# Converting the first weights 1024 wide without GpSimd, and squaring on ScalarE alone

## The chip, the core and the metric

One core of a Trainium2 chip. The metric is the time of one execution on the device in microseconds. An engine's queue runs in order; the program gives each engine its own order, and semaphores hold an instruction until its inputs are written and its output buffer is free.

## The reference

Three layers in a row on 3072 tokens of 512 features:

```python
# retention: per token t and head, decay gamma_h = 1 - 2^(-5-h)
state = gamma * state + outer(k[t], v[t]);  y[t] = scale * q[t] @ state
# first MLP, d_ff = 2048
r = maximum(x @ w_in, 0);  x2 = (s * r * r + b) @ w_out
# second MLP: 8 experts, each takes exactly 384 tokens by sorted gate logits
out[mask] = maximum(x2[mask] @ w1[e], 0) @ w2[e]
```

The outputs are compared as float32. The weights `w_in` and `w_out` of the first MLP are drawn as float64 and not cast, so they come to the chip as 64-bit words (`w64`, seen as int64), and the kernel has to make 32-bit numbers of them.

## The kernel before

Float32 products are made from two rounded parts: each operand is split into a high part (`fp32r`) and the remainder, and three matmuls (high x high, high x low, low x high) stand for one.

**Weights of the first MLP.** `w64` holds 16 features (slices of 128 of `d_ff`), each with two pieces of 128 x 512 words (`w_in`, `w_out`): 32 pieces `n`, feature `f = n // 2`. `conv_load` (line 228) fetches a piece of 512 KB into one of six buffers, on SP's queue. `conv_gen` (line 233) converts one piece at a time: from the upper word `hi32` VectorE takes the exponent shifted by three bits (line 262), joins the sign (266), sets very small numbers to zero with the help of a square made by ScalarE (239, 269), takes the bare power of two (275) and multiplies it by the lower word (279). For the piece before, ScalarE rounds the number to the high part `h` (249), GpSimd subtracts (251) and adds the lower word's share to give the low part `l` (253). Each `yield` tells a planner (`Weave`, `Side`) how much time the step is charged (`CY`); the planner issues a step when its due time has come, between the units of TensorE's work. `conv_until` forces conversion forward when a unit needs weights that are not yet issued.

**Order.** At first three blocks of 256 tokens go through the retention (`attn`, six chunks of 128 tokens), with a few pieces of conversion in between (`PRO`, `PN`). The chunks' loads and the first raw pieces stand on SP's queue in the order written near line 571. VectorE masks (344) and makes remainders (377), GpSimd scales each chunk by decays (201, 204). Then the *wide* stage: `moe1((0, 1, 2), ...)` takes feature by feature, and for each the three blocks. A *unit* is `h_unit` (12 matmuls, line 425, 256 wide, then `relu` on ScalarE into `r`, line 428) and, two units later, `x_unit` (six matmuls, line 458, 512 wide). Conversion runs beside it. Then comes the *narrow* stage: blocks 3 to 9 one after the other with the next block's retention and the gate logits (line 481) beside them; then the last two blocks as a pair (`h_pair`), and after that the expert stage.

**Squares.** `r_split` makes the two parts of `r * r`. In the wide stage ScalarE squares and rounds in one instruction (436), VectorE makes the unrounded square from `r` and the accumulator bank `ph` (440), GpSimd subtracts (441). In the later stages `low_parts` issues VectorE's square (447) and its subtraction (448) at the start of the next unit.

Buffers: `tmp` has six, used by conversion and by the logits; `loads` holds the later chunks of q, k and v in `q0` and `q2`, two of each, where the raw pieces lie as well; `stage` has two `sa` and two `sb`.

Of the kernel before, what the change touches and what calls it, by code (L numbers as in the profile page):

```python
# [35 lines left out]
TINY_WORD = 1.125 * 2.0 ** -15  # L36
# [45 lines left out]
def kernel(  # L82
# [19 lines left out]
    CY=(560, 890),  # L102
# [72 lines left out]
    def load_chunk(j):  # L175
        if j < CPB:

            ts = []
            for i in range(4):
                n = 2 * NF - 1 - 2 * j - i // 2  # L180
                tag = ("h", "l")[i % 2] + str(n)
                ts.append(wpool.tile([128, 512], F32, name=f"first{j}_{i}", tag=tag))
            for i in (0, 1, 3, 2):
                SP.dma_start(ts[i], qkv[j, :, i])
                if j == 0 and i in first:
                    first[i]()
            if j:
                load_dec(j)
        else:
            ts = []  # L190
            load_dec(j)
            for i in (0, 2):
                t = loads.tile([128, 2, 512], F32, name=f"q{i}", tag=f"q{i}")
                SP.dma_start(t, qkv[j, :, i:i + 2])
                ts += [t[:, 0, :], t[:, 1, :]]
        QKV[j] = ts
# [28 lines left out]
    NRAW = 6  # L225
    READY = set()

    def conv_load(n):
        pool, tag = ((stage, "sa"), (loads, "q0"), (loads, "q2"))[n // 2 % 3]
        RAW[n] = pool.tile([128, 512], I64, name="raw", tag=tag)  # L230
        SP.dma_start(RAW[n], w64[n // 2, n % 2])

    def conv_gen():
        sq = {}

        def square(n):
            hf = RAW[n].bitcast(F32).rearrange("p (n t) -> p t n", t=2)[:, 1, :]
            sq[n] = tmp.tile([128, 512], F32, name="tmp")
            ACT.activation(sq[n], hf, AF.Square)

        square(0)
        last = None

        def parts(step):
            n, a, p = last
            if step == 0:
                W[n] = (wpool.tile([128, 512], F32R, name=f"h{n}", tag=f"h{n}"),
                        wpool.tile([128, 512], F32R, name=f"l{n}", tag=f"l{n}"))
                ACT.activation(W[n][0], a, AF.Copy)
            elif step == 1:  # L250
                POOL.tensor_tensor(a, a, W[n][0].bitcast(F32), op=OP.subtract)
            else:
                POOL.tensor_tensor(W[n][1], a, p, op=OP.add)  # L253
                READY.add(n)

        for n in range(2 * NF):
            raw = RAW.pop(n)
            hi32 = raw.bitcast(I32).rearrange("p (n t) -> p t n", t=2)[:, 1, :]
            lo32 = raw.bitcast(U32).rearrange("p (n t) -> p t n", t=2)[:, 0, :]
            a = tmp.tile([128, 512], F32, name="tmp")  # L260
            ai = a.bitcast(I32)
            DVE.tensor_scalar(ai, hi32, 3, 0x3FFFFFFF, op0=OP.logical_shift_left, op1=OP.bitwise_and)  # L262
            if last:
                parts(0)
            yield CY[0]
            DVE.scalar_tensor_tensor(ai, hi32, -0x40000000, ai, op0=OP.bitwise_and, op1=OP.bitwise_or)  # L266
            yield CY[1]
            p = sq.pop(n)
            DVE.scalar_tensor_tensor(a, p, TINY_WORD * TINY_WORD, a, op0=OP.is_ge, op1=OP.mult)  # L269
            if last:  # L270
                parts(1)
            if n + 1 < 2 * NF:
                square(n + 1)
            yield CY[1]
            DVE.tensor_scalar(p.bitcast(I32), ai, -0x800000, None, op0=OP.bitwise_and)
            yield CY[0]
            if last:
                parts(2)
            DVE.scalar_tensor_tensor(p, lo32, 2.0 ** -52, p, op0=OP.mult, op1=OP.mult)
            if n + NRAW < 2 * NF:  # L280
                conv_load(n + NRAW)
            last = (n, a, p)
            yield CY[1]
        for step in range(3):
            parts(step)
            yield 600
# [129 lines left out]
    def h_unit(blk, f, hb):  # L416
# [12 lines left out]
        return r, ph  # L429
# [3 lines left out]
    def r_split(r, rh, rl, ph=None):  # L433


        ACT.activation(rh, r, AF.Square)  # L436
        if ph is None:
            LOW.append((r, rh, rl))
        else:
            DVE.scalar_tensor_tensor(r, ph, 0.0, r, op0=OP.max, op1=OP.mult)  # L440
            POOL.tensor_tensor(rl, r, rh.bitcast(F32), op=OP.subtract)
        return rh, rl

    def low_parts():
        while LOW:
            r, rh, rl = LOW.pop(0)
            DVE.tensor_tensor(r, r, r, op=OP.mult)  # L447
# [96 lines left out]
    def moe1(blks, xbs, lag, apart=0):  # L544
# [5 lines left out]
        for n in range(len(seq) + lag):  # L550
            if n < len(seq):
                def hu(n=n):
                    f, i = seq[n]
                    conv_until(2 * f + 1)
                    low_parts()
                    r, ph = h_unit(blks[i], f, 2 + n % 2)
                    R2[blks[i], f] = r_split(r, work.tile([128, TB], F32R, name="rh", bufs=3),
                                             work.tile([128, TB], F32R, name="rl", bufs=3),
                                             ph if len(blks) > 1 else None)
# [14 lines left out]
    conv_load(1)  # L574
    SP.dma_start(sb[:, 0:1], bass.AP(tensor=moe_s.tensor, offset=moe_s.offset, ap=[[0, 128], [1, 1]]))
    SP.dma_start(sb[:, 1:2], bass.AP(tensor=moe_b.tensor, offset=moe_b.offset, ap=[[0, 128], [1, 1]]))
    for j in range(2, CPB):
        load_chunk(j)
        conv_load(j)
# [19 lines left out]
    conv_until(2 * NF - 1)  # L599
# [62 lines left out]
    def h_pair(f):  # L662
        rs = []
        for i, blk in enumerate(pair):
            wv.unit(1320, lambda: rs.append(h_unit(blk, f, 2 + i)[0]))
# [512 lines left out]
```

## Time and profile before

| | us |
|---|---|
| median of three runs | 1146.67 (1144.25 to 1148.87) |
| the profiled execution | 1142.75 |
| its span, first to last instruction | 1141.0 |
| TensorE busy in the span | 1016.3 |
| VectorE busy | 875.2 |
| ScalarE busy | 385.1 |
| GpSimd busy | 221.7 |

Busy time is a mean over stages with different limits; what an edit is worth is read in its own stage. Waiting for a semaphore is shown as idle time ahead of an instruction; anything that holds an instruction after its start is inside its duration, so the shortest and the mean duration of one line are read together.

### The profile page before, as it was taken

The numbers are of one execution on the slowest core, as the hardware profiler recorded it, in microseconds if no ns is written. First come the engines' busy times: TensorE is split into PE (matmuls) and PEld (weight loads), VectorE is DVE, ScalarE is ACT, GpSimd is POOL, SyncE is SP. The second block draws the span as 40 slices with busy tenths as digits, with TensorE's granted clock in tenths as the row PEclk, the third lists the DMA queues.
The fourth block names the chain that finished last, engine by engine and source line by source line (L and its number), as shares of the span: only waits on it lengthen the run. The fifth ranks groups of instructions, "written<-read, shape, count | busy, mean of one in ns | idle before, by whom it ended". The sixth has DMA issues, their size and how long they took to land.

```text
span 1141.0 us, 19761 instructions
## 1 busy us (share of the span) xinstructions
PE 1016.3 (89%) x7636; PEld 875.8 (77%) x7636; DVE 875.2 (77%) x2114; ACT 385.1 (34%) x802; POOL 221.7 (19%) x211
## 2 busy tenths in 40 slices
PE   5887877899999999999998999578789888888997
PEld 4766666788889898989897888467677677776786
DVE  3899999669999999999964744667787787867642
ACT  2433333332323323223333331223333443333442
POOL 3777777620000000000000000010111102011211
PEclk8999999999999999999999999869799999999999
DMA  9422222262212121221121000322333333343540
GB/s 323 144 90 92 93 93 82 96 193 75 66 47 75 56 57 56 57 74 58 35 95 32 2 1 11 138 66 85 120 102 121 111 108 134 95 133 116 166 139 28
DMA packets 35040, 104.51 MB, mean 92 GB/s; under 512 B 4737, under 2 KB 5249, under 8 KB 34945
## 3 DMA queue, kind: packets, MB, share of 16 engines
q1 hardware_dynamic: 30528, 89.60, 24.2%
q0 software_dynamic: 3840, 12.59, 3.3%
q8 instruction: 60, 0.98, 0.3%
q10 hardware_dynamic: 576, 1.05, 0.3%
q14 instruction: 36, 0.29, 0.1%
HBM read 90.64 MB, written 12.58 MB: 90 GB/s over the span
## 4 chain that ended last, share of the span: by engine, by line
PE 55%; DVE 23%; issue 11%; DMA 5%; ACT 2%; POOL 2%; SPq 0%; POOLq 0%; DVEq 0%; ACTq 0%
PE b L425 17%; PE b L458 13%; PE b L1012 6%; PE b L1033 5%; PE b L687 3%; DVE tmp L262 3%; DMA big<-x2d,idx 3%; DVE l L990 2%; PE b L794 2%; PE b L358 2%; PE b L368 2%; DVE tmp L266 2%; PE b L338 2%; DVE tmp L269 2%; DVE cmp L787 2%
## 5 line engine op out<-in xcount | busy, mean ns | idle before, releaser
L425 PE MATMUL b<-xh,h 128*128 128x256 f32 x704 | 201.7, 287 | 22.6 <-DVE r L440 20.9
L481 DVE SCALAR_TENSOR_TENSOR scr<-tmp,wg 128x512 bf16<-128x512 f32 x288 | 198.3, 689 | 6.8 <-ACT tmp L468 1.8
L425 PE MATMUL b<-xh,l 128*128 128x256 f32 x704 | 199.5, 283 | 0.9 <-POOL l L253 0.9
L425 PE MATMUL b<-xl,h 128*128 128x256 f32 x704 | 199.3, 283 | 0.0
L425 PEld LDWEIGHTS b<-xh,h 128*128 128x128 f32 x704 | 134.4, 191 | 39.2 <-DVE r L440 31.1
L428 ACT ACTIVATE r<-b 128x256 f32<-128x256 f32 x192 | 73.2, 382 | 253.3 <-PE b L425 225.5
L425 PEld LDWEIGHTS b<-xl,h 128*128 128x128 f32 x704 | 134.4, 191 | 4.8
L425 PEld LDWEIGHTS b<-xh,l 128*128 128x128 f32 x704 | 134.6, 191 | 1.5 <-POOL l L253 1.5
L458 PE MATMUL b<-h,rh 128*128 128x512 f32 x320 | 130.3, 407 | 0.0
L458 PE MATMUL b<-h,rl 128*128 128x512 f32 x320 | 127.1, 397 | 2.7 <-DVE rl L448 2.7
L458 PE MATMUL b<-l,rh 128*128 128x512 f32 x320 | 127.4, 398 | 0.0
L950 POOL DMA_INDIRECT big<-x2d,idx x24 | 26.1, 1088 | 355.1 <-issue 152.6
L1012 PE MATMUL b<-gh,h 128*128 128x384 f32 x256 | 93.1, 364 | 0.0
L1033 PE MATMUL b<-h,hh 128*128 128x512 f32 x192 | 81.0, 422 | 13.3 <-ACT hh L1015 13.3
L1012 PE MATMUL b<-gl,h 128*128 128x384 f32 x256 | 88.2, 344 | 1.7 <-DVE gl L962 1.7
L1012 PE MATMUL b<-gh,l 128*128 128x384 f32 x256 | 87.8, 343 | 0.0
L990 DVE TENSOR_TENSOR l<-eraw,h 128x512 fp32r<-128x512 f32 x128 | 82.3, 684 | 6.6 <-ACT h L989 6.6
L1033 PE MATMUL b<-h,hl 128*128 128x512 f32 x192 | 78.9, 411 | 8.0 <-DVE hl L1021 7.8
L447 DVE TENSOR_TENSOR r<-r 128x256 f32<-128x256 f32 x144 | 60.7, 421 | 25.6 <-ACT h L436 17.9
L1015 ACT ACTIVATE hh<-b 128x384 fp32r<-128x384 f32 x64 | 31.3, 489 | 138.3 <-PE b L1012 138.3
L1033 PE MATMUL b<-l,hh 128*128 128x512 f32 x192 | 76.9, 401 | 0.0
L458 PEld LDWEIGHTS b<-h,rl 128*128 128x128 f32 x320 | 61.0, 191 | 19.3 <-DVE rl L448 5.5
(193 smaller groups left out, 2054.2 us busy)
## 6 DMA issues: line engine op xcount, KB each, us to landing
eraw<-in_w_dram SPq DMA_DIRECT2D x64, 512.0 KB, 3.6
q<-in_qkv_dram SPq DMA_DIRECT2D x36, 512.0 KB, 4.7
raw<-in_w_dram SPq DMA_DIRECT2D x32, 512.0 KB, 3.5
first<-in_qkv_dram SPq DMA_DIRECT2D x24, 256.0 KB, 6.0
qdec<-in_dec_dram SPq DMA_DIRECT2D x24, 256.0 KB, 2.7
x2d<-tmp SPq DMA_DIRECT2D x20, 256.0 KB, 3.8
wg<-in_wgT_dram SPq DMA_DIRECT2D x4, 512.0 KB, 3.6
x2d<-tmp ACTq DMA_DIRECT2D x4, 256.0 KB, 2.0
```

Of the source, the lines that this page charges most:

```text
L262: DVE.tensor_scalar(ai, hi32, 3, 0x3FFFFFFF, op0=OP.logical_shift_left, op1=OP.bitwise_and)
L425: PE.matmul(ph, a[:, ks], b[:, kc, :], start=(n == 0), stop=(n == 3 * KC - 1))
L428: ACT.activation(r, ph, AF.Relu)
L447: DVE.tensor_tensor(r, r, r, op=OP.mult)
L458: PE.matmul(X2[blk][t], a[:, ts], b, start=(f == 0 and i == 0), stop=(f == NF - 1 and i == 2))
L481: DVE.scalar_tensor_tensor(scr, x, 1.0, WG[e], op0=OP.mult, op1=OP.mult, accum_out=of[:, e:e + 1])
L687: PE.matmul(XB[c], a[:, cs], b, start=(f == 0 and i == 0), stop=(f == NF - 1 and i == 2))
L950: POOL.indirect_dma_start(out=xg[:, t, :], out_offset=None, in_=x2d[:, :], in_offset=bass.IndirectOffsetOnAxis(ap=IDX[i][:, t:t + 1], axis=0))
L990: DVE.tensor_tensor(lo, raw[:, a, :], hi.bitcast(F32), op=OP.subtract)
L1012: PE.matmul(PH[0], a[:, ks], b[:, kc, :], start=(kc == 0 and n == 0), stop=(kc == KC - 1 and n == 2))
L1015: ACT.activation(hh, PH[0], AF.Relu)
L1033: PE.matmul(Y[i, t], a[:, ts], b, start=(f == 0 and j == 0), stop=(f == NF2 - 1 and j == 2))
```

## The change

The conversion handles a whole feature (both pieces, 1024 wide) at a time. ScalarE gives the magnitude (`Abs`), VectorE clamps, shifts, joins and makes the lower word's share in place in the raw tile, ScalarE rounds two halves, and VectorE does the subtractions and additions that GpSimd did. Raw features lie in the two buffers of `q`, now one tile of 8 KB for each partition; the first loads and the planner's charges change with it. ScalarE squares `r` in place and rounds it in a second instruction, in all stages; VectorE only subtracts.

```diff
-TINY_WORD = 1.125 * 2.0 ** -15
+ZERO_WORD = 2.0 ** -15
-    CY=(560, 890),
+    CY=(700, 1200, 650),
# load_chunk, chunks from 6 on
+            t = loads.tile([128, 4, 512], F32, name="q")
             for i in (0, 2):
-                t = loads.tile([128, 2, 512], F32, name=f"q{i}", tag=f"q{i}")
-                SP.dma_start(t, qkv[j, :, i:i + 2])
-                ts += [t[:, 0, :], t[:, 1, :]]
+                SP.dma_start(t[:, i:i + 2], qkv[j, :, i:i + 2])
+                ts += [t[:, i, :], t[:, i + 1, :]]
-    def conv_load(n):
...
+    def conv_load(f):
+        RAW[f] = loads.tile([128, 1024], I64, name="raw", tag="q")
+        for i in range(2):
+            SP.dma_start(RAW[f][:, i * 512:(i + 1) * 512], w64[f, i])
     def conv_gen():
...
+        def magnitude(f):
+            mag[f] = stage.tile([128, 1024], F32, name="c", tag="sa")
+            ACT.activation(mag[f], RAW[f].bitcast(F32).rearrange("p (n t) -> p t n", t=2)[:, 1, :], AF.Abs)
+        magnitude(0)
+        for f in range(NF):
+            raw = RAW.pop(f)
+            (_, hi), (_, hf), (lo, _), (lf, _) = (
+                [v[:, t, :] for t in range(2)] for v in
+                (raw.bitcast(d).rearrange("p (n t) -> p t n", t=2) for d in (I32, F32, U32, F32)))
+            c = mag.pop(f)
+            ci = c.bitcast(I32)
+            DVE.tensor_scalar(c, c, ZERO_WORD, None, op0=OP.max)
+            yield CY[0]
+            DVE.tensor_scalar(ci, ci, 3, 0x3FFFFFFF, op0=OP.logical_shift_left, op1=OP.bitwise_and)
+            yield CY[0]
+            DVE.scalar_tensor_tensor(hi, hi, -0x40000000, ci, op0=OP.bitwise_and, op1=OP.bitwise_or)
+            for i in range(2):
...
+                ACT.activation(W[n][0], hf[:, i * 512:(i + 1) * 512], AF.Copy)
+            yield CY[1]
+            DVE.tensor_scalar(ci, hi, -0x800000, None, op0=OP.bitwise_and)
             yield CY[0]
+            DVE.scalar_tensor_tensor(lf, lo, 2.0 ** -52, c, op0=OP.mult, op1=OP.mult)
             yield CY[1]
+            for i in range(2):
+                h, l = W[2 * f + i]
+                part = slice(i * 512, (i + 1) * 512)
+                DVE.tensor_tensor(hf[:, part], hf[:, part], h.bitcast(F32), op=OP.subtract)
+                yield CY[2]
+                DVE.tensor_tensor(l, hf[:, part], lf[:, part], op=OP.add)
+                if f + 1 < NF and not i:
+                    magnitude(f + 1)
+                yield CY[2]
+            if f + 2 < NF:
+                conv_load(f + 2)
+            READY.add(f)
# squares
-    def r_split(r, rh, rl, ph=None):
-        ACT.activation(rh, r, AF.Square)
-        if ph is None:
-            LOW.append((r, rh, rl))
-        else:
-            DVE.scalar_tensor_tensor(r, ph, 0.0, r, op0=OP.max, op1=OP.mult)
-            POOL.tensor_tensor(rl, r, rh.bitcast(F32), op=OP.subtract)
+    def r_split(r, rh, rl):
+        ACT.activation(r, r, AF.Square)
+        ACT.activation(rh, r, AF.Copy)
+        LOW.append((r, rh, rl))
     def low_parts():
         while LOW:
             r, rh, rl = LOW.pop(0)
-            DVE.tensor_tensor(r, r, r, op=OP.mult)
             DVE.tensor_tensor(rl, r, rh.bitcast(F32), op=OP.subtract)
# first loads
     conv_load(0)
     load_chunk(1)
-    conv_load(1)
...
     for j in range(2, CPB):
         load_chunk(j)
-        conv_load(j)
+        if j == 3:
+            conv_load(1)
```

`conv_until(2 * f + 1)` becomes `conv_until(f)`, and `PN = 2` now means feature 2 and no longer piece 2.

## Rows read from the trace of the kernel before

**Rows 1.** The page, busy tenths in 40 slices of 28.5 us, by engine

```profile
PE   5887877899999999999998999578789888888997
DVE  3899999669999999999964744667787787867642
POOL 3777777620000000000000000010111102011211
```

**Rows 2.** Stretches: us, busy PE, PEld, DVE, ACT, POOL (instructions), clock, DMA, GB/s

```profile
47.00:212.00 165.00, 133.23 (x762) 108.92 (x762) 161.55 (x182) 65.22 (x139) 127.03 (x97) 0.97 0.29 93
239.00:600.00 361.00, 360.05 (x2702) 324.05 (x2703) 324.36 (x866) 113.22 (x273) 1.49 (x2) 1.00 0.22 68
600.00:645.00 45.00, 39.85 (x325) 35.05 (x324) 28.71 (x76) 14.64 (x39) 1.22 (x4) 1.00 0.06 20
```

**Rows 3.** Waits from 47 to 215 us: waiter, cause: total us, times, longest

```profile
ACT tmp L239 <- POOL l L253: 60.6, 26, 3.8
PEld b L425 <- DVE r L440: 47.2, 36, 2.5
```

**Rows 4.** Groups from 47 to 215 us: busy us, mean ns, idle before, releasers

```profile
L253 POOL TENSOR_TENSOR l<-tmp 128x512 fp32r<-128x512 f32 x29 | 46.1, 1591 | 1.0
...
L279 DVE SCALAR_TENSOR_TENSOR tmp<-raw,tmp 128x512 f32<-128x512 uint32 x29 | 35.8, 1234 | 0.8
L269 DVE SCALAR_TENSOR_TENSOR tmp<-tmp 128x512 f32<-128x512 f32 x29 | 35.0, 1208 | 0.6
...
L262 DVE TENSOR_SCALAR tmp<-raw 128x512 int32<-128x512 int32 x28 | 33.2, 1184 | 0.0
L266 DVE SCALAR_TENSOR_TENSOR tmp<-raw,tmp 128x512 int32<-128x512 int32 x28 | 28.9, 1034 | 0.8
...
L275 DVE TENSOR_SCALAR tmp<-tmp 128x512 int32<-128x512 int32 x29 | 22.1, 762 | 0.7
L249 ACT ACTIVATE h<-tmp 128x512 fp32r<-128x512 f32 x29 | 18.3, 632 | 35.9 <-DVE tmp L269 35.9
L239 ACT ACTIVATE tmp<-raw 128x512 f32<-128x512 f32 x27 | 18.3, 678 | 60.6 <-POOL l L253 60.6
L436 ACT ACTIVATE rh<-r 128x256 fp32r<-128x256 f32 x43 | 18.0, 418 | 1.4
...
L428 ACT ACTIVATE r<-b 128x256 f32<-128x256 f32 x43 | 15.9, 371 | 3.2 <-PE b L425 3.1
```

**Rows 5.** Single lines, whole span: duration min/median/max; page's group of line 990

```profile
L262 DVE TENSOR_SCALAR tmp<-raw x32: 410/1162/1517, 20.0 to 208.5; 128x512 int32<-128x512 int32 x32
L266 DVE SCALAR_TENSOR_TENSOR tmp<-raw,tmp x32: 674/902/1672, 21.1 to 209.5; 128x512 int32<-128x512 int32 x32
L448 DVE TENSOR_TENSOR rl<-r,rh x112: 424/425/428, 242.0 to 619.2; 128x256 fp32r<-128x256 f32 x112
L990 DVE TENSOR_TENSOR l<-eraw,h 128x512 fp32r<-128x512 f32 x128 | 82.3, 684 | 6.6 <-ACT h L989 6.6
```

**Rows 6.** Timeline, TensorE, the wide stage's first matmul: start, duration

```profile
46.88 0.39 PE L425 MATMUL b<-xh,h 128*128 128x256 f32 x1 [1.41 <-DVE xls L377]
```

**Rows 7.** Chain and timeline at the end of the wide stage, TensorE

```profile
219.16 1.43 PE b L425 x12
...
224.81 1.45 PE b L425 x12
...
230.28 1.16 PE L338 MATMUL b<-q 64*128 64x128 f32 x16
232.11 1.16 PE L338 MATMUL b<-q 64*128 64x128 f32 x16 [0.67 <-POOL q L201]
```

**Rows 8.** Timeline, ScalarE, the only load of function tables

```profile
0.75 1.28 ACT L376 ACT_TABLE_LOAD   x1 [0.75 <-PEq L1165]
```

**Rows 9.** The raw tile, whole span: from issue to landing

```profile
DMA to landing us min/median/max: 3.3/3.5/8.4
```

**Rows 10.** Waits from 583 to 650 us

```profile
PEld b L674 <- DVE l L448: 2.9, 4, 1.4
```

## Blind prediction

> **What bounds the kernel now.** I read the slices of the page first, then a table by stage, then, for the one stage that stands out, the groups by line and the waits. The slices show TensorE at seven or eight tenths until about 228 us, with VectorE at nine from 57 to 200 us and GpSimd at seven; from 240 to 600 us TensorE is at nine [rows 1]. [...] So two stages have two limits. From 47 us on the "wide" stage runs (three token blocks against each feature's weights, while VectorE still converts the weights) and there VectorE is the bound: TensorE's largest wait is on VectorE's `r` of line 440, 47 us in total, and ScalarE sits 61 us behind GpSimd's sums of line 253 [rows 3]. In the later, narrow stage TensorE is the bound.
>
> Why VectorE is full is seen in the groups and in the spread of single lines. Line 262 takes 0.41 us at best and 1.18 us on average in this stage, line 266 0.67 at best, 1.67 at worst and 1.03 on average [rows 4, 5]. The same instruction on the same shape is thus two to three times as long at times, and the time it gains is about that of a GpSimd instruction (1.59 us, line 253) [rows 4]. I read it so: an instruction of VectorE that meets a GpSimd one waits for it inside its own duration.
>
> The wide stage on TensorE starts at 46.88 us [rows 6] and ends where the next stage's line 338 starts, 230.28 us [rows 7]: 183.4 us. When conversion is over, one unit (12 matmuls of line 425 and six of line 458) takes (224.81 - 219.16) / 2 = 2.82 us [rows 7], so 48 units are 135.4 us of TensorE. The most that can be won here is 48 us.
>
> **The change part by part.** *Conversion on VectorE.* Per feature it now issues three one-source instructions, two two-source ones, all 1024 wide, and four subtractions or additions 512 wide. A two-source instruction takes 0.425 us at 256 wide and 0.684 at 512 [rows 5], so 0.26 us for 256 more. The one-source line 262 does 512 in 0.41, that is 512 elements in the time of 256; 1024 wide it is 0.41 + 0.26 = 0.67 us. Two-source at 1024: 0.674 + 0.52 = 1.19 us. Sum: 3 x 0.67 + 2 x 1.19 + 4 x 0.684 = 7.13 us. Before, a feature was ten instructions 512 wide, with GpSimd beside them 2 x (1.18 + 1.03 + 1.21 + 0.76 + 1.23) = 10.8 us [rows 4]. In the wide stage GpSimd now has nothing to do (lines 251, 253 and 441 are gone), so I take the shortest durations, not the means.
>
> *Squares.* Line 440 and GpSimd's line 441 go; ScalarE squares in place and then rounds; VectorE keeps one subtraction of 0.425 us for each unit, issued at the start of the next unit, where its inputs are long ready. TensorE's bank is now released by ScalarE's `relu` alone, which removes the 47 us wait as such; what comes late next is the subtraction, which the second product needs two units later.
>
> *The sum of the wide stage.* The planner charges 7100 for a feature's conversion and 7860 for its three units, so the conversion runs ahead: when the remaining 14 features are through, 14 x 7100 / 2620 = 38 of the 48 units have been issued. VectorE until then: 1.4 us (the last subtractions of feature 1) + 14 x 7.13 + 38 x 0.425 = 117.4 us. Neighbours that don't depend on each other overlap by some 0.07 us; I take 3.5 us off for that and put 2.1% idle on, as in [rows 2] (161.55 of 165): 116.3 us. Ten units are left, 28.2 us, of which TensorE, waiting for the subtraction of two units earlier, can already be ahead by up to 4; I take 2. Together 116.3 + 26.2 = 142.5 us instead of 183.4: 40.9 us less.
>
> *ScalarE.* Per feature: magnitude 1024 wide, about 2 x 0.68 less one start, 1.1 to 1.35 us; two rounded parts, 1.26; three units at 0.37 + 0.42 + 0.42, 3.6 [rows 4]. About 6.1 us in a feature of 8.3: not a bound. A load of function tables is seen once, 1.28 us [rows 8]; I count none for the new function; if it needed its own, 2 x 1.28 us a feature would put ScalarE at 8.7 and cost 14 x 0.4 = 6 us.
>
> *Loads.* Only two raw features are held instead of three, and the load of feature f+2 waits on SP for the last addition of feature f. Behind it on SP stand the next raw loads, and at the end chunks 6 and 7, which take the buffers of features 14 and 15: free near 163 us, wanted near 190. That a later chunk is one tile with two loads costs nothing: both halves were freed and loaded together before. The magnitude on ScalarE, and with it `relu` behind it, waits for the landing. A raw half lands 3.5 us after issue at the median and 8.4 at worst [rows 9]; two issued 0.4 us apart, at about 4 to 5.5, then 1.1 to 1.35 us of magnitude: 6.9 at most, against 8.3 us for a feature. Hidden, at nothing; the rival below prices the worst.
>
> *Start.* The conversion's wider instructions stand between the masks of the attention on VectorE. In program order a 1024-wide pair (0.67 + 1.19) comes ahead of the masks of chunks 2 and 4 and the evictions after them, where half as much came before; the rounded parts stand ahead of an eviction on ScalarE. GpSimd's conversion work leaves its queue, so the last chunk's scaling comes earlier, and chunks 3 and 5 are loaded 512 KB sooner, chunk 1 later; feature 2's load now waits for feature 0, after all the chunks. Between -2 and +3 us; I take +1.5, nearer to the instructions that are certain.
>
> *Later stages.* In the narrow stage 112 multiplications of VectorE (line 447) go, each about as long as line 448's 0.425 us [rows 5], 48 us in all, and 112 roundings of ScalarE come. TensorE is at 360 of 361 us there [rows 2], so this brings nothing; without that cover it would be up to 48 us. Where the last pair of blocks begins TensorE idles 5.15 of 45 us [rows 2], in part behind VectorE's subtraction [rows 10]; with 0.84 us less on VectorE per feature I take 1.8 us. GpSimd's scaling of chunks 6 and 7 no longer queues behind line 441: the 0.67 us wait [rows 7] goes.
>
> Sum: -40.9 + 1.5 - 0.7 - 1.8 = -41.9 us. From the profiled execution, 1142.75 us (span 1141.0), that gives 1100.9. It lies 3.9 us under the median of the runs, so against the median 1146.67 the forecast is 1104.8: 1105 us.
>
> **The rivals.** *TensorE takes over.* If the overlap is larger than I take and no idle comes, VectorE needs no more than TensorE; then the stage is 135.4 us plus the first unit's start, about 1, and the time is 1146.67 - 47 + 1.5 - 2.5 = 1099. For it: 7.13 + 1.28 = 8.41 us against 8.46 a feature. Against: the planner sets conversion ahead, 8.3 us in 7100 of its units.
>
> *The raw load shows.* With landings at the 8.4 us that a row shows, a feature takes 8.4 + 0.4 + 1.1 = 9.9 us instead of 8.3: 14 x 1.6 = 22 us, and the time is 1127. For it: no third buffer. Against: the median 3.5.
>
> *Writes at every second word are slow.* Four instructions of a feature (the join, the lower word's share, two subtractions) now write into the raw tile in place, at every second word, 3072 elements together. No row shows such a write. Reads of this kind cost nothing: line 266 reads at every second word in 0.674 us. Bounds for 512 such elements: nothing more (that row), or 1.00 us more (the same line at its worst, 1.67). I take nothing, since reading and writing walk the same words. At 0.50 us more for each 512 (six a feature, 14 features, 42 us) the gain is used up: at 0.52, each step doubled, 1149, no change; at 1.00, 84 us longer, 1189, slower.
>
> [...]
>
> **How the numbers follow.** Forecast 0.62 (1096 to 1113), TensorE's rival 0.13, the load's 0.14, slow writes 0.11 (of which 0.04 lands within 0.5%). The range from 1093 to 1127 takes in the first three and leaves out slow writes. Half a percent, 5.7 us, is about what a measurement of this kernel can tell from no change. Faster 0.89, same 0.04, slower 0.07.
>
> **What the profile of after would show.** Line by line in the wide stage: one-source conversion at 0.67, two-source at 1.19, subtractions at 0.68 us, minimum and median alike; longer ones at the raw tile's writes alone mean slow writes. GpSimd idle from 50 us to the end of the wide stage. VectorE over 95% busy until about 163 us; if it idles on ScalarE's magnitude, the load shows. The first matmul of line 338 in the next stage near 191 us. From there on the same distances as before. The forecast is wrong if that start comes after 205 us, or if the narrow stage, which now has ScalarE's extra rounding, no longer holds TensorE at full.

## The result and the profile after

| | before | after |
|---|---|---|
| median, us | 1145.46 (1141.52 to 1148.87, four runs) | 1106.49 (1105.77 to 1107.8, four runs) |
| ratio | 1 | 0.9662, 95% interval 0.9628 to 0.9696 |
| span of the profiled execution | 1141.0 | 1104.3 |
| wide stage, start to end | 46.88 to 230.28: 183.4 | 51.83 to 191.96: 140.1 |

The change makes the kernel 3.4% faster; the forecast was 1105 us. Lines of after: 237 is the magnitude, 248, 250, 253, 261 and 263 are VectorE's conversion in the order of the diff, 258 the rounding, 268 and 270 the subtraction and addition; 415, 418, 426, 427, 434 and 444 are `h_unit`'s matmul, `relu`, the square, its rounding, VectorE's subtraction and `x_unit`'s matmul. The attention's matmuls are at 328 and 348, its masks at 334, the eviction at 366 and 367.

The page's slices of after, busy tenths in 40 slices of 27.6 us, answer [rows 1]:

```profile
PE   5699999899999999999999998596888898888997
...
DVE  2899992587887878787726243777868787876642
...
POOL 3200010000000000000000000102020201111211
```

TensorE reaches nine tenths from the third slice on, where before it stood at seven and eight until 228 us; from 36.5 us on GpSimd stands still until it scales chunks 6 and 7, from 161.7 us on. The table of stretches, with busy time of TensorE, weight loads, VectorE, ScalarE and GpSimd (instructions in brackets), granted clock, DMA share and GB/s, answers [rows 2]:

```profile
52.00:98.00 46.00, 46.00 (x302) 42.14 (x303) 44.40 (x67) 30.93 (x66) 0.00 (x0) 1.00 0.40 138
98.00:166.00 68.00, 65.84 (x406) 56.41 (x406) 66.42 (x98) 44.23 (x94) 3.52 (x2) 1.00 0.38 132
166.00:192.00 26.00, 26.00 (x162) 23.07 (x160) 5.94 (x13) 13.34 (x31) 2.47 (x2) 1.00 0.35 118
192.00:204.00 12.00, 8.74 (x122) 7.66 (x121) 4.52 (x9) 3.23 (x8) 2.45 (x2) 0.86 0.65 202
204.00:565.00 361.00, 361.00 (x2708) 326.92 (x2709) 281.24 (x755) 158.76 (x383) 0.21 (x1) 1.00 0.21 66
565.00:610.00 45.00, 41.74 (x346) 37.70 (x346) 23.34 (x62) 22.59 (x59) 1.24 (x4) 1.00 0.07 21
```

The wide stage has three parts now. To 98 us TensorE never idles. To 166 us VectorE is full (66.4 of 68) and TensorE loses 2.2 us to it. From 166 us on conversion is over, VectorE rests, and TensorE alone sets the pace. The stage of 140.1 us thus stands 4.7 us above the 135.4 us that TensorE needs. From 204 to 565 us TensorE is full as it was before. From 192 to 204 us it works only 8.7 of 12.

The conversion's own lines, shortest, median and longest duration in ns, answer [rows 5]; a reader compares the three figures of a line with each other:

```profile
L258 ACT ACTIVATE h<-raw x32: 652/674/707, 26.5 to 161.0; 128x512 fp32r<-128x512 f32 x32
L268 DVE TENSOR_TENSOR raw<-raw,h x32: 680/686/1787, 33.2 to 166.0; 128x512 f32<-128x512 f32 x32
...
L237 ACT ACTIVATE c<-raw x16: 1122/1147/1173, 21.6 to 154.9; 128x1024 f32<-128x1024 f32 x16
L253 DVE SCALAR_TENSOR_TENSOR raw<-raw,c x16: 1217/1226/2168, 24.3 to 159.2; 128x1024 int32<-128x1024 int32 x16
L261 DVE TENSOR_SCALAR c<-raw x16: 683/692/695, 29.0 to 160.7; 128x1024 int32<-128x1024 int32 x16
...
DMA to landing us min/median/max: 3.4/4.3/7.9
```

Shortest and median lie within 4% of each other: what was stretched in [rows 4, 5] is stretched no more. The longest ones lie where GpSimd still scales a chunk: line 253 took 2.17 us at 24.29 us, and line 268 took 1.79 us at 162.55 us, beside the scaling of chunk 6.

Where the 36.7 us between the two spans lie, stretch by stretch, from the first matmul of each stage:

| stretch | before | after | difference |
|---|---|---|---|
| to the start of the wide stage | 46.88 | 51.83 | +4.95 |
| wide stage | 183.4 | 140.1 | -43.3 |
| from its end to the narrow stage | 8.56 | 11.89 | +3.3 |
| the rest | 902.2 | 900.5 | -1.7 |

### The profile page after: what moved, and what is told of

The parts are those of the page before. It is cut to its first block, busy times and chain, and to the rows that moved or that the text cites. A ratio compares the mean times of both kernels' runs of the same rounds, so it can differ in the third digit from the quotient of the medians.

```text
span 1104.3 us, 19566 instructions
## 1 busy us (share of the span) xinstructions
PE 1006.6 (91%) x7636; PEld 877.4 (79%) x7636; DVE 769.6 (70%) x1954; ACT 460.6 (42%) x978; POOL 78.0 (7%) x99
## 4 chain that ended last, share of the span: by engine, by line
PE 66%; DVE 15%; issue 8%; DMA 6%; ACT 3%; POOL 2%; SPq 0%; POOLq 0%; DVEq 0%; ACTq 0%
PE b L415 22%; PE b L444 18%; PE b L997 6%; PE b L1018 5%; PE b L672 3%; DMA big<-x2d,idx 3%; PE b L779 2%; DVE l L975 2%; PE b L348 2%; PE b L358 2%; PE b L328 2%; DVE cmp L772 2%; POOL big L935 2%; DVE raw L268 1%; DVE raw L253 1%
## 5 line engine op out<-in xcount | busy, mean ns | idle before, releaser
L434 DVE TENSOR_TENSOR rl<-r,rh 128x256 fp32r<-128x256 f32 x160 | 68.7, 430 | 46.7 <-ACT rh L427 46.2
L426 ACT ACTIVATE r<-r 128x256 f32<-128x256 f32 x192 | 79.9, 416 | 5.1
```

The costliest lines, as they stand in the source:

```text
L426: ACT.activation(r, r, AF.Square)
L434: DVE.tensor_tensor(rl, r, rh.bitcast(F32), op=OP.subtract)
```

## The experiments

The theory was the prediction's: GpSimd beside VectorE stretches VectorE's instructions, the squares take 0.42 us of VectorE in each unit, and both together bound the wide stage. Rivals were that one part carries all, and that GpSimd's time is no loss but help. Medians are set against runs of before on the same chip, by ratio; where two kernels ran on different chips, their ratios compare better than their medians (that of before was 1142.7 to 1144.9 us on the four chips).

| label | edit, in short | us | ratio (95%) | wide stage, us |
|---|---|---|---|---|
| x1_squares | before, new squares alone | 1127.7 | 0.9858 (0.9835 to 0.988) | 173.0 |
| x12_nopool | before, GpSimd out of the conversion | 1121.7 | 0.9809 (0.9768 to 0.9851) | 160.9 |
| x4_pieces | both of these, still 512 wide | 1100.8 | 0.963 (0.9608 to 0.9652) | 146.1 |
| x11_pieces_new | x4 with the change's arithmetic | 1090.2 | 0.9537 (0.9511 to 0.9563) | 137.4 |
| x2_conversion | after, old squares | 1145.4 | 1.001 (0.9996 to 1.0024) | 173.5 |
| x8_coupled | x2, VectorE subtracts instead of GpSimd | 1148.8 | 1.0044 (1.0015 to 1.0072) | 175.9 |
| x9_vsquare | after, VectorE squares in `low_parts` | 1130.8 | 0.9884 (0.986 to 0.9909) | 160.3 |
| x3_pool | after, 268 and 270 on GpSimd | 1122.1 | 0.9798 (0.9782 to 0.9815) | 155.4 |
| x5_halves | after, chunk 8's halves freed apart | 1103.0 | 0.9642 (0.9615 to 0.9669) | 140.1 |
| x6_start | after, conversion later in the start | 1105.9 | 0.9681 (0.9665 to 0.9697) | 142.5 |
| x13_order | after, chunk 1 loaded ahead of feature 0 | 1103.2 | 0.9656 (0.9619 to 0.9693) | 140.2 |

### The squares alone

```diff
# on before, r_split and low_parts
-        ACT.activation(rh, r, AF.Square)
-        if ph is None:
-            LOW.append((r, rh, rl))
-        else:
-            DVE.scalar_tensor_tensor(r, ph, 0.0, r, op0=OP.max, op1=OP.mult)
-            POOL.tensor_tensor(rl, r, rh.bitcast(F32), op=OP.subtract)
+        ACT.activation(r, r, AF.Square)
+        ACT.activation(rh, r, AF.Copy)
+        LOW.append((r, rh, rl))
...
-            DVE.tensor_tensor(r, r, r, op=OP.mult)
```

> The kernel before with the squares of the change alone (ScalarE squares and rounds, VectorE only subtracts); the conversion stays 512 wide with GpSimd. Theory (VectorE's time in the wide stage sets it, and GpSimd stretches VectorE): a feature cost VectorE 10.8 us where its shortest durations sum to 5.7, a stretch of 5.1 us beside 9.3 us of GpSimd; now GpSimd has 6.4 us a feature, so the stretch is about 3.5, VectorE 5.7 + 3.5 + 1.3 = 10.5 us against 11.6 to 12; the wide stage shrinks by 14 x 1.1 to 1.5 = 15 to 21 us, later stages by 2: about 1126, ratio 0.983. Rival (TensorE's bank, held by VectorE's line 440, is what cost the 47 us wait, and the squares free it): 35 to 40 us, about 1108, ratio 0.967, and nothing is left for the conversion.

Measured: 1127.7 us, 1.4% faster. The groups of VectorE from 52 to 160 us (busy us, mean ns, idle before them):

```profile
L262 DVE TENSOR_SCALAR tmp<-raw 128x512 int32<-128x512 int32 x19 | 28.9, 1522 | 0.0
L266 DVE SCALAR_TENSOR_TENSOR tmp<-raw,tmp 128x512 int32<-128x512 int32 x19 | 26.6, 1403 | 0.5
...
L275 DVE TENSOR_SCALAR tmp<-tmp 128x512 int32<-128x512 int32 x20 | 8.5, 424 | 0.4
```

Lines 262 and 275 are the same operation on the same shape, 1.52 us and 0.42 us. Both engines in order of time show why, first GpSimd's two instructions of a piece, then VectorE's:

```profile
98.85 1.80 POOL L251 TENSOR_TENSOR tmp<-tmp,h 128x512 f32<-128x512 f32 x1 [2.43 <-ACT h L249]
100.74 1.36 POOL L253 TENSOR_TENSOR l<-tmp 128x512 fp32r<-128x512 f32 x1
```

```profile
99.42 1.52 DVE L262 TENSOR_SCALAR tmp<-raw 128x512 int32<-128x512 int32 x1
100.98 1.67 DVE L266 SCALAR_TENSOR_TENSOR tmp<-raw,tmp 128x512 int32<-128x512 int32 x1
102.75 0.69 DVE L269 SCALAR_TENSOR_TENSOR tmp<-tmp 128x512 f32<-128x512 f32 x1
```

Each of the two stretched ones begins while one of GpSimd's runs and ends 0.3 to 0.6 us after it; the next one is short again. With line 441 gone the stretch of 262 and 266 did not get less; lines 269, 275 and 279 lost it (0.74, 0.42 and 0.69 us on average), so that the five of a piece take 4.78 us on average instead of 5.42 [rows 4], while the squares' subtraction (444) is now stretched too, 0.68 us for 0.42. The squares are worth 16 us by themselves and don't carry the result.

### GpSimd's part alone, and both at 512 wide

```diff
# on before, conv_gen
-                POOL.tensor_tensor(a, a, W[n][0].bitcast(F32), op=OP.subtract)
+                DVE.tensor_tensor(a, a, W[n][0].bitcast(F32), op=OP.subtract)
...
-                POOL.tensor_tensor(W[n][1], a, p, op=OP.add)
+                DVE.tensor_tensor(W[n][1], a, p, op=OP.add)
```

This alone is x12_nopool; with the edit of x1_squares on top it is x4_pieces.

> The kernel before with the two GpSimd instructions of a conversion piece moved to VectorE and nothing else: pieces 512 wide, the old arithmetic, the old squares (VectorE behind each unit, GpSimd subtracts). With x4_pieces it shows what the squares do once GpSimd is out of the conversion. Theory (VectorE behind each unit idles, and GpSimd's one subtraction still stretches): VectorE 8.46 + 2.7 x 0.41 + 1.3 idle + about 1.3 stretch = 12.2 us a feature against 11.6 to 12: no gain or slower, 1143 to 1155. Rival (taking GpSimd out of the conversion is the gain, the squares add their own): about 1120.

> The squares of the change, and the two GpSimd instructions of a piece moved to VectorE; pieces stay 512 wide with the old arithmetic, GpSimd idle in the wide stage. Theory: no stretch left; VectorE per feature 5.7 + 4 x 0.684 + 1.3 = 9.7 us, so until the conversion ends 14 x 8.46 + 40 x 0.425 = 135 us, then 7 or 8 units, 20 us: 154 us in place of 183; later stages 2.5 less: about 1114, ratio 0.973. Rival (the width and the shorter arithmetic bring the gain; taking GpSimd out merely moves work to the full engine): as the squares alone or slower, 1126 and up.

Measured: x12_nopool 1121.7 us. VectorE was full, was given two more instructions for each piece, and the kernel became 1.9% faster. My expectation of 1143 to 1155 was wrong and its rival right. The same view of x12_nopool, and its stretch from 98 to 160 us:

```profile
L251 DVE TENSOR_TENSOR tmp<-tmp,h 128x512 f32<-128x512 f32 x22 | 19.4, 882 | 0.0
...
L440 DVE SCALAR_TENSOR_TENSOR r<-b,r 128x256 f32<-128x256 f32 x31 | 12.9, 416 | 0.0
...
L262 DVE TENSOR_SCALAR tmp<-raw 128x512 int32<-128x512 int32 x21 | 8.7, 414 | 0.0
```

```profile
98.00:160.00 62.00, 53.84 (x320) 44.31 (x321) 61.42 (x105) 28.83 (x61) 16.78 (x18) 1.00 0.35 108
```

Line 262 is back at its shortest, 0.41 us. What is still stretched (line 251, 0.88 where 0.68 is its unstretched size) lies beside line 441 of GpSimd, which this kernel keeps.

x4_pieces came to 1100.8 us, below what the theory gave it (1114). The shares of the two parts, 1.4 and 1.9%, add up to 3.3%, and together they give 3.7% (3.5 to 3.9): they add, as far as the intervals tell. VectorE's groups of x4_pieces in the same stretch:

```profile
L262 DVE TENSOR_SCALAR tmp<-raw 128x512 int32<-128x512 int32 x25 | 10.6, 422 | 0.0
L266 DVE SCALAR_TENSOR_TENSOR tmp<-raw,tmp 128x512 int32<-128x512 int32 x25 | 18.3, 730 | 0.7
```

So the whole gain is had without the width, with the old arithmetic. What follows: GpSimd's leaving and the squares are enough for the gain of the change; a feature at a time, 1024 wide, is not needed for it.

### The change's arithmetic in pieces

```diff
# on x4_pieces
-            ACT.activation(sq[n], hf, AF.Square)
+            ACT.activation(sq[n], hf, AF.Abs)
...
-            DVE.tensor_scalar(ai, hi32, 3, 0x3FFFFFFF, op0=OP.logical_shift_left, op1=OP.bitwise_and)
+            p = sq.pop(n)
+            DVE.tensor_scalar(p, p, ZERO_WORD, None, op0=OP.max)
...
+            DVE.tensor_scalar(ai, p.bitcast(I32), 3, 0x3FFFFFFF, op0=OP.logical_shift_left, op1=OP.bitwise_and)
...
-            p = sq.pop(n)
-            DVE.scalar_tensor_tensor(a, p, TINY_WORD * TINY_WORD, a, op0=OP.is_ge, op1=OP.mult)
```

> The squares of the change, no GpSimd, pieces 512 wide in six buffers as in x4_pieces, but the arithmetic of the change: magnitude by ScalarE, clamp, shift and join, so that a 0.67 us instruction of each piece becomes one of 0.41. VectorE 7.9 us a feature for conversion against 8.5 in x4_pieces and 7.1 in the changed kernel. Theory (VectorE's time paces the second half of the wide stage; the start and the stage's end stay as with pieces): the wide stage 139 to 141 us in place of 146, start and transition as in x4_pieces: 1095. Rival (VectorE has room enough, what is left are waits between engines): 1100, as x4_pieces.

Measured: 1090.2 us, the fastest of all, and its interval lies wholly below that of after. Its stretches of the wide stage, and the first matmul of the stage (start, duration, and in brackets the wait and what ended it):

```profile
45.00:98.00 53.00, 53.00 (x346) 48.41 (x345) 52.36 (x110) 37.55 (x85) 0.00 (x0) 1.00 0.39 122
98.00:160.00 62.00, 62.00 (x397) 56.15 (x396) 61.31 (x123) 42.91 (x96) 5.12 (x4) 1.00 0.42 135
```

```profile
44.43 0.39 PE L425 MATMUL b<-xh,h 128*128 128x256 f32 x1 [1.41 <-DVE xls L377]
```

TensorE is full in both stretches and the stage takes 137.4 us, 2 above its floor. A compare-and-multiply with two sources has become a maximum with one, some 0.26 us less (0.68 to 0.42) for each of 32 pieces, 8 us; the stage is 8.7 us shorter than in x4_pieces and starts 1.2 us earlier, 9.9 of the 10.6 us between the two. Against after it gains 7.4 us at the start, 2.7 in the stage, and the rest behind it. Width, buffers, load order and the planner's charges differ between these two; only the load order and the tile's halves were tried by themselves (below), so which of the others costs how much stays open.

### The change with the old squares

```diff
# on after, r_split
-        ACT.activation(r, r, AF.Square)
-        ACT.activation(rh, r, AF.Copy)
-        LOW.append((r, rh, rl))
+        ACT.activation(rh, r, AF.Square)
+        if ph is None:
+            LOW.append((r, rh, rl))
+        else:
+            DVE.scalar_tensor_tensor(r, ph, 0.0, r, op0=OP.max, op1=OP.mult)
+            POOL.tensor_tensor(rl, r, rh.bitcast(F32), op=OP.subtract)
...
+            DVE.tensor_tensor(r, r, r, op=OP.mult)
```

> The changed kernel with the old squares: VectorE makes the unrounded square (0.41 us) and GpSimd subtracts in the wide stage; VectorE squares and subtracts in the later stages. Theory: GpSimd is back with 2.9 us a feature, which stretches VectorE by about 1.6; with 7.1 + 1.2 that is 10 us a feature; the wide stage about 158 to 162 us in place of 140, the later stage 1.9 longer: about 1128, ratio 0.985 to the kernel before. Rival (the squares carry the gain): 1140 or more. Rival (GpSimd's subtraction finds gaps, no stretch): 1109.

Measured: 1145.4 us, nothing gained; the theory's 1128 was wrong. The number of the first rival (1140 or more) came, but not its reason: x1_squares shows that the squares alone bring 16 us. x12_nopool has the same squares and gained 22 us, so the old squares are harmful beside the wide conversion in a way that they are not beside pieces. The waits from 52 to 160 us (us in total, times, longest):

```profile
ACT h L258 <- DVE raw L253: 49.8, 10, 6.2
PEld b L415 <- DVE r L430: 24.5, 16, 3.4
DVE r L430 <- ACT rh L426: 13.1, 9, 2.1
```

and two views in order of time, VectorE's and ScalarE's:

```profile
120.21 1.23 DVE L253 SCALAR_TENSOR_TENSOR raw<-raw,c 128x1024 int32<-128x1024 int32 x1
...
123.50 0.42 DVE L430 SCALAR_TENSOR_TENSOR r<-b,r 128x256 f32<-128x256 f32 x1 [2.06 <-ACT rh L426]
```

```profile
121.47 1.21 ACT L258 ACTIVATE h<-raw 128x512 fp32r<-128x512 f32 x2 [5.16 <-DVE raw L253]
122.58 0.37 ACT L418 ACTIVATE r<-b 128x256 f32<-128x256 f32 x1
122.98 0.42 ACT L426 ACTIVATE rh<-r 128x256 fp32r<-128x256 f32 x1
```

It is a ring of queues that run in order. ScalarE holds two roundings and has waited 5.16 us for VectorE's join (253), because in the wide conversion the rounding is issued right behind the join of the same feature. The unit's `relu` (418) and square (426) stand behind the roundings. VectorE's square of that unit (430) needs both and stands at the head of VectorE's queue: VectorE, the engine that is short, stands still for 2.06 us, and TensorE's bank stays taken (24.5 us of waits). With pieces the rounding belongs to the piece before and needs an earlier result. It waits for VectorE there too (line 249 in x12_nopool: 33.5 us in 21 waits from 52 to 160 us), but 2.5 us at most, and VectorE has no idle time ahead of line 440, as the row of x12_nopool shows.

### The place of VectorE's square, and its price

x8_coupled is x2_conversion with VectorE's subtraction, so that GpSimd is out of the wide stage; x9_vsquare does VectorE's same two instructions, but both deferred to the start of the next unit.

```diff
# x8_coupled, on x2_conversion
-            POOL.tensor_tensor(rl, r, rh.bitcast(F32), op=OP.subtract)
+            DVE.tensor_tensor(rl, r, rh.bitcast(F32), op=OP.subtract)
# x9_vsquare, on after
-        ACT.activation(r, r, AF.Square)
-        ACT.activation(rh, r, AF.Copy)
+        ACT.activation(rh, r, AF.Square)
...
+            DVE.tensor_tensor(r, r, r, op=OP.mult)
```

> The changed kernel with VectorE's old squares in the wide stage and its subtraction instead of GpSimd's, both issued right behind each unit: no GpSimd at all in the wide stage. VectorE has 7.13 + 2.7 units x 0.84 = 9.4 us a feature. Theory (an instruction on VectorE that reads the unit's accumulator stops VectorE until TensorE and ScalarE are through, while TensorE's bank waits for VectorE): VectorE idles 1.3 us a feature as in the run with the old squares and GpSimd, 10.7 us a feature, and the wide stage stays near 173 us: 1142 to 1146. Rival (it was GpSimd's subtraction that spoiled that run): no idle on VectorE, wide stage about 162 us, 1128.

> The changed kernel with VectorE's own square (r times r, 0.42 us a unit) put back ahead of its subtraction, both issued at the start of the next unit in all stages, ScalarE squaring and rounding in one instruction; no GpSimd. The same work on VectorE as in x8_coupled, 9.4 us a feature, but nothing on VectorE waits for TensorE. Theory: VectorE stays over 97% busy, wide stage 1.4 + 14 x 7.13 + 38 x 0.84 + 26 = 159 to 162 us, later stages 1.8 longer: 1126 to 1130. Rival (the squares' place, not their time on VectorE, is all): 1107 to 1109. Rival (VectorE's time is all, the place nothing): the same time as x8_coupled.

Measured: 1148.8 and 1130.8 us, both just above the theory's ranges. From 98 to 160 us, x8_coupled and then x9_vsquare:

```profile
98.00:160.00 62.00, 49.75 (x283) 41.69 (x282) 52.70 (x86) 24.25 (x48) 0.00 (x0) 0.94 0.29 102
```

```profile
98.00:160.00 62.00, 54.88 (x324) 44.79 (x324) 59.06 (x97) 28.21 (x57) 0.00 (x0) 1.00 0.30 103
```

GpSimd is at zero in both, so the loss of x2_conversion does not need GpSimd. (In x2_conversion its subtraction still stretched VectorE, line 263 to 1.39 us and 270 to 0.84; in x8_coupled VectorE does that subtraction itself, 0.43 us a unit.) The same work of VectorE costs 18 us more where it stands behind each unit and waits there (9.3 of 62 us idle) than deferred (2.9 idle). The granted clock is 0.94 against 1.00 in this stretch. How much of the 18 us that adds was not told apart. The second figure is between x9_vsquare and after: 0.42 us of VectorE less for each of 48 units is worth 24 us. In the wide stage it is 20.2 us, as much as the 48 x 0.42 = 20 us of work itself; 2.6 us more lie in the start. Both together, 42 us, are what the new squares are worth beside the wide conversion; beside pieces they were worth 16 to 21.

### GpSimd put back

```diff
# on after, conv_gen
-                DVE.tensor_tensor(hf[:, part], hf[:, part], h.bitcast(F32), op=OP.subtract)
+                POOL.tensor_tensor(hf[:, part], hf[:, part], h.bitcast(F32), op=OP.subtract)
...
-                DVE.tensor_tensor(l, hf[:, part], lf[:, part], op=OP.add)
+                POOL.tensor_tensor(l, hf[:, part], lf[:, part], op=OP.add)
```

> The changed kernel with the four subtractions and additions of a feature (lines 268 and 270) given back to GpSimd. VectorE has 4 x 0.684 = 2.7 us less a feature to do. Theory (GpSimd stretches VectorE more than it relieves it): 4.4 us of conversion, stretched by 0.55 us for each of GpSimd's 6.4 us, 3.5, and 1.3 for the squares: 9.2 us against 8.4; the wide stage 5 to 12 us longer: about 1114, with the one-source instructions' mean well over their 0.69. Rival (no stretch, work merely divides): VectorE has 5.7 us a feature, TensorE bounds the whole stage: 1101.

Measured: 1122.1 us. VectorE has four instructions of 0.69 us a feature less to do, and the kernel is 15.6 us slower than after. The groups from 52 to 160 us:

```profile
L248 DVE TENSOR_SCALAR c<-c 128x1024 f32<-128x1024 f32 x12 | 17.7, 1476 | 5.7 <-ACT c L237 5.6
...
L434 DVE TENSOR_TENSOR rl<-r,rh 128x256 fp32r<-128x256 f32 x31 | 28.0, 911 | 2.5 <-ACT rh L427 2.5
```

Line 248 goes from 0.69 to 1.48 us on average, line 434 from 0.42 to 0.91: the squares' subtraction alone gives back 31 x 0.49 = 15 us in this stretch, lines 248, 250 and 263 some 20 us more. The instructions given to GpSimd would have been about 32 us of VectorE there. The theory had 1114; the stretch of the short instructions was larger than I sized it. A second cost is new: line 248 waits 5.6 us for the magnitude, and the magnitude 5.4 us for raw loads to land. I read it so, without a run that shows it: GpSimd's later additions free the raw tiles later, and so the next loads start later. Which share of the 15.6 us is which was not told apart.

### Chunk 8's halves

```diff
# on after, load_chunk
-            t = loads.tile([128, 4, 512], F32, name="q")
+            t = QT[j] = QT.pop(j - 2) if j - 2 in QT else loads.tile([128, 4, 512], F32, name="q")
```

The tile of chunk 6 is used again as it is, so each half is waited for by itself.

> The changed kernel, with chunks from 8 on loaded into the same tile as two chunks earlier instead of a newly taken one, so that the half with q and k waits for the readers of that half alone, as with the two tiles of the kernel before. Theory (the one tile of a chunk holds chunk 8's q and k back until all of chunk 6 is read): the load of chunk 8's first half starts about 3 us sooner, TensorE's wait of 3.1 us behind GpSimd's scaling goes, and the stretch from the end of the wide stage to the first matmul of block 3 falls from 12.0 to about 8.6 us: 1103. Rival (the wait is the loads of the gate's weights in front on SP's queue): 1106.5, unchanged.

Measured: 1103.0 us, as expected. TensorE's first matmuls behind the wide stage, after and then x5_halves:

```profile
191.96 2.06 PE L328 MATMUL b<-q 64*128 64x128 f32 x32
...
201.84 2.08 PE L328 MATMUL b<-q 64*128 64x128 f32 x16 [3.13 <-POOL q L201]
```

```profile
195.34 2.06 PE L329 MATMUL b<-q 64*128 64x128 f32 x32
...
202.21 1.16 PE L329 MATMUL b<-q 64*128 64x128 f32 x16
```

The wait of 3.13 us is gone, and chunk 8's scores follow 6.9 instead of 9.9 us after the stage's end. The medians differ by 3.4 us, the ratios by 2.3, with intervals that overlap; the wait in the trace is the firmer evidence. Why it came is seen on SP's queue, the load of chunk 8 before and then after:

```profile
231.50 3.66 SPq L194 DMA_DIRECT2D q<-in_qkv_dram  x2
```

```profile
196.12 0.80 SPq L194 DMA_DIRECT2D q<-in_qkv_dram  x2
```

Before, the first load is issued 1.2 us after the wide stage's end, the second 3.3 us later (the 3.66 us reach to that one's end): the half with q and k was free as soon as the scores of chunk 6 had read it. In after both loads start together, 4.2 us after the end; in x5_halves the first goes 1.2 us after it again. The late load had a second cost: behind the wait the granted clock was 0.50 (from 201.8 to 206 us), with 0.41 us for a matmul of line 415 instead of 0.28. In x5_halves, without the wait, the same matmuls took 0.28 us.

### The start

Two edits try what makes the start longer: the conversion's steps placed later by the planner, and chunk 1's load ahead of the first raw feature on SP's queue.

```diff
# x6_start, on after
-    conv.due = 3000.0
+    conv.due = 5500.0
# x13_order, on after
-    conv_load(0)
     load_chunk(1)
+    conv_load(0)
```

> The changed kernel with the conversion's first due time at 5500 instead of 3000, so that feature 0 is begun after the eviction of chunk 1 and its last steps come after the masks of chunk 2. Theory (the start is 5 us longer because 1024-wide instructions and their rounded parts stand ahead of chunk 1's eviction and chunk 2's masks): TensorE's wait of 5.0 us for the masks of chunk 2 falls to under 2, the wide stage starts at about 48.5 instead of 51.8 us, and some 2 us of conversion move into the wide stage, which has little room: 1104. Rival (the later arrival of chunk 1 and the loads set the start): unchanged within 1 us, 1106.5.

> The changed kernel with the first loads in another order: chunk 1 ahead of the two halves of raw feature 0. Theory A (the later arrival of chunk 1, 16.7 in place of 15.2 us, carries through the start): chunk 1's first matmul at about 13.7 us, the wide stage starts 2 to 3 us earlier, 1104. Theory B (the start is held by VectorE's conversion ahead of chunk 2's masks, and that begins when chunk 1's eviction is through): as A, since both move. Rival (the masks of chunk 2 wait for feature 0, whose raw tile now lands later): no change, 1106.

What they are to change is this wait of TensorE in after, with VectorE's queue ahead of it:

```profile
31.57 2.36 PE L348 MATMUL b<-am,first 128*64 128x128 f32 x15 [4.98 <-DVE am L334]
```

```profile
24.29 2.17 DVE L253 SCALAR_TENSOR_TENSOR raw<-raw,c 128x1024 int32<-128x1024 int32 x1
...
28.36 0.69 DVE L367 SCALAR_TENSOR_TENSOR xl<-b,xh 128x512 fp32r<-128x512 f32 x1 [1.91 <-ACT xh L366]
28.97 0.68 DVE L261 TENSOR_SCALAR c<-raw 128x1024 int32<-128x1024 int32 x1
29.69 1.23 DVE L263 SCALAR_TENSOR_TENSOR raw<-raw,c 128x1024 f32<-128x1024 uint32 x1
30.83 2.48 DVE L334 TENSOR_TENSOR am<-b,mask 128x512 f32<-128x512 f32 x4
```

The masks of chunk 2 (334) stand behind feature 0's conversion, the stretched join first of all. Ahead of them VectorE also waits 1.91 us for ScalarE's eviction, which stands behind the two roundings, which wait for that join, as in x2_conversion. Measured: x6_start 1105.9 us, no change that the medians show (by ratio 2 us slower, intervals overlapping); its theory was wrong. The wait for the masks fell to 3.84 us only, a wait of 2.52 us on ScalarE's `sbd` came later, and the wide stage took 2.4 us more. x13_order 1103.2 us: chunk 1's first matmul came at 14.19 instead of 16.70 us, the masks' wait was 2.67 us, and the wide stage began at 49.22:

```profile
14.19 2.08 PE L328 MATMUL b<-first,first 64*128 64x128 f32 x16 [6.08 <-POOL first L201]
...
49.22 0.39 PE L415 MATMUL b<-xh,h 128*128 128x256 f32 x1 [1.41 <-DVE xls L367]
```

The load order is thus part of it in the trace, while by ratio x13_order is only 0.7 us faster than after and the intervals overlap. The trace gives the 2.6 us of the start in two parts: VectorE begins feature 0 1.7 us sooner (line 248 at 21.13 instead of 22.83 us), and the join meets no scaling of GpSimd there (1.23 us instead of 2.17).

A single profile's start is good to 2 or 3 us: kernels with the same start as after began the wide stage between 51.8 and 55.2 us. The traces show what goes with it. The five instructions of feature 0 ahead of the masks (248, 250, 253, 261, 263) take 4.5 us unstretched, as in x13_order, 5.5 in after, where one meets GpSimd's scaling, and 7.1 to 7.9 in x9_vsquare, x2_conversion, x5_halves and x8_coupled, where three or four do. TensorE's wait for the masks goes the same way: 2.7, 5.0 and 7.4 to 8.1 us.

## Why the prediction was right, and where it was not

*The bound was read rightly.* VectorE, stretched by GpSimd, bounded the wide stage. x12_nopool shows it without any other edit, x3_pool the reverse. Single instructions show it too: in x1_squares one operation on one shape takes 1.52 us in line 262 and 0.42 in line 275, and the long one begins while an instruction of GpSimd runs. That VectorE waits inside that duration was my reading; the traces show the duration and not what holds it. The prediction put the time that a stretched instruction gains at about that of a GpSimd one; it is less, 1.1 us for line 262 beside 1.4 to 1.8, as VectorE's begins while GpSimd's runs.

*Durations.* One source 1024 wide: 0.67 forecast, 0.69 measured; two sources: 1.19 and 1.226; subtractions 0.684 and 0.69. A feature is 3 x 0.69 + 2 x 1.226 + 4 x 0.69 = 7.28 us instead of 7.13. ScalarE's magnitude at 1.15 us lies in the bounds given, and no second table load is seen. GpSimd, forecast idle to the end of the wide stage, was not: its scaling of chunk 6 stretched lines 268 and 434 at 162.5 to 165.5 us by some 2 us together.

*The wide stage.* 142.5 us forecast, 140.1 measured. VectorE's part was forecast at 116.3 us and ended 115.6 us after the stage's start. What followed took 24.5 us instead of 26.2: of the 28.2 us counted for ten units TensorE had done 3.7 us already, where I took 2. The end of the stage, 191.96, came within 1 us of the 191 named.

*The rivals.* Slow writes fall: line 268 in place at every second word takes 0.686 us, as long as the 0.684 of line 990, of the same width [rows 5], and line 253's 1.226 leaves them no more than 3% over the 1.19 worked out. The load's rival falls too: a median of 4.3 us, 7.9 at worst, and a single wait of 1.2 us for the magnitude, in the start. TensorE's rival was nearly met in the stage (140.1 against its 136.4).

*The start was mis-sized.* I took +1.5 with bounds of -2 and +3; the profiles show +5 to +8 in kernels with this start. The step that failed is the one that counted only the extra instructions ahead of the masks. Chunk 1's later arrival, which the prediction named, is 1.5 us (its first matmul at 16.70 instead of 15.15). The step left out that the join meets GpSimd's scaling there (0.95 us more in after, more in other profiles) and that it then holds the roundings, the eviction behind them, and VectorE's next instruction behind that.

*"That a later chunk is one tile with two loads costs nothing: both halves were freed and loaded together before" was wrong.* They were not: SP's queue of before shows 3.3 us between them. From the wide stage's end to the narrow stage I forecast -0.7 and +3.3 came. x5_halves takes the wait away.

*Later.* TensorE 361 of 361 in the narrow stage, as forecast. In 565 to 610 us its idle time fell from 5.15 to 3.26 us: 1.9, with 1.8 forecast.

*The sum.* -41.9 forecast and -36.7 measured between the spans: 3.5 at the start and 4.0 behind the stage were missed, and 2.4 in the stage were given back. That the time, 1105 forecast and 1106.5 measured, came closer than these terms is luck: an error in the stage set off a part of the others, the median of before fell by 1.2 us to 1145.5 with its fourth run, and its profiled execution lies 2.7 us under that, so that the medians differ by 39.0 us where the spans differ by 36.7.

*The reason was right only in part.* I spoke of the width as part of the gain (512 elements in the time of 256). x4_pieces and x11_pieces_new show that the gain doesn't need it: pieces do at least as well, and 16 us better with the change's shorter arithmetic. And I said of the squares that the wait on line 440 goes "as such" and that the subtraction is next; that beside the wide conversion the old squares would undo all of the gain was not in the prediction, and I missed it again in what I expected of x2_conversion and, turned round, of x12_nopool.

*Open.* The 2 or 3 us between x13_order, x5_halves and after are not resolved by the medians, and why GpSimd's scaling meets one instruction of feature 0 in one profile and four in another was not tried. Whether x11_pieces_new gains from x13_order's load order was not tried.

## What to carry to other kernels

Where one line's shortest duration is far below its mean and the long ones lie beside a second engine's instructions, moving that engine's work onto the full one can make the kernel faster (here 0.41 and 1.18 us for line 262, and 22 us won by the move alone, in x12_nopool). Before making instructions wider, look what is queued behind the larger step on each engine in the ring (here the rounding ahead of `relu`), and whether the gain isn't had with small ones. When two tiles become one, ask when each half was freed, not only when both were full.

## What the runs showed of the chip that I had not expected

Every second word of a tile, read and written in place, cost VectorE nothing that shows: 0.686 us against 0.684 for 512 (lines 268 and 990), 1.226 for 1024 with two sources (line 253). The stretch beside GpSimd fell on the instruction that begins while one of GpSimd's runs: with GpSimd's two instructions a piece in x1_squares on the one-source line 262 (1.52 us on average, against 0.42 in x4_pieces), with GpSimd's short one in x12_nopool on the two-source lines alone (line 251 0.88 us, line 262 0.41). Line 440, whose other source is an accumulator bank, was not stretched: 0.41 to 0.43 us in all 48 cases of before, also at 126.12 us, within a run of GpSimd's line 253 (125.73 to 127.34). And a full VectorE took on 64 instructions of 0.85 to 0.88 us in that kernel, which became 22 us faster.
